# A polysketch attention and ELU kernel: one transpose placed five steps earlier, one outer product with a factor in PSUM, two of GpSimd's four sums in one operation

## The chip, the core and the metric

The kernel runs on one core of one Trainium2 chip. The metric is the time of one execution on the device in microseconds, taken as the median over runs. A core has these engines, each with its own instruction queue that is worked off in order: TensorE (PE in the profile, with its weight loads as PEld), VectorE (DVE), ScalarE (ACT), GpSimd (POOL), and SyncE (SP), which here only issues DMAs. They are tied together by semaphores: an instruction waits until the results and the buffers that it needs are there.

## What is computed

The reference, cut to what matters:

```python
batch, n_heads, seq, head_dim, r = 4, 4, 1088, 32, 8
def phi(x):                                   # 64 features of each row
    a = einsum('rd,bhsd->bhsr', S1, x)
    b = einsum('rd,bhsd->bhsr', S2, x)
    return einsum('bhsi,bhsj->bhsij', a, b).reshape(..., 64)
q_p, k_p = phi(q), phi(k)
kv = einsum('bhsf,bhsd->bhfd', k_p, v);  z = sum(k_p, axis=2)
num = einsum('bhsf,bhfd->bhsd', q_p, kv)
x = num / (einsum('bhsf,bhf->bhs', q_p, z) + 1e-6)
x = x.transpose(0, 2, 1, 3).reshape(4352, 128)    # heads side by side
h = x @ w_in                                      # 128 -> 2048
g = where(h > 0, h, exp(min(h, 0)) - 1)
out = g @ w_out                                   # 2048 -> 128
```

q, k and v are float32 in memory, S1, S2 and the weights float64 (two 32-bit words each). The kernel turns those to float32 itself as it needs them.

## The kernel before

**Two halves that run interleaved.** The second half, the two matrix products with the ELU between them, is most of the work. Its tokens are cut into nine groups g of 512 (the last one of 256), its 2048 hidden columns into eight pairs cp of 2 x 128. A step is one pair (g, cp). The list `steps` (lines 951 to 953) gives the order, and the loop at lines 1047 to 1087 works it off with the number n. The first half, the attention, supplies the input `xg` of each group just in time: its pieces hang on chosen steps.

**One step n** does, in the order of the instructions: `mm1` of (g, cp), two tiles `h` of 128 x 512 in PSUM; the extras given with `at(n, ...)`; `elu` of the first tile (on ScalarE `e` = relu(-h), then exp(-e), lines 808 and 810; on VectorE `gg` = max(e - 1, h), line 816); GpSimd's sums for it (`sums7`, c = 0); the extras given with `mid`; `elu` of the second tile; its sums (`sums7`, c = 1); the extras given with `late`; and last the second product of step n-2, `mm2`, `mm2_blocks` or `mm2_seven`. So a tile `gg` and its sums are used two steps after they are made. In steps where a group ends, that product comes ahead of the second `elu`.

**The seven products.** From group 2 on, and for two pairs of group 1, the second product is done with seven block products in place of eight (`mm2_seven`, line 723). It needs sums of the quarters of `gg`: with b11 and b12 the two halves of the first tile, b21 and b22 those of the second, GpSimd makes t0 = b12 - b11, t2 = b22 - b12, t1 = t2 + b11 and t3 = b21 - t1, each of 128 x 256 elements, in the tile `tt`. `SS` holds the matching sums of weights, made once by `weights7`. Most steps use the order t0, t2, t1, t3; the first and the last pair of a group use t1 first.

**The queries of a group** take this way, spread over steps: `transp` (line 279) transposes a batch's queries on VectorE from `hd_q` to `qT`; `queries(g5, g1, n)` (line 655) is one block of small matmuls on TensorE, the last product `q5` of group g5 and the first, `q1`, of group g1, into the two `h` tiles that the next step's `mm1` would use and two tiles `qps`; `q1_out` (line 541) brings q1's result to `abw` on VectorE; `q2_den` (line 555) makes the denominator and `an`, the first factor of the features divided by it, in four VectorE operations (`pw`, `den` twice, `an`; lines 560 to 570); `q2_half` (line 620) makes the outer product `qp` of `an` and the second factor; `q4` (line 628) transposes it to `qpT`, which `q5` uses. `q2_a` (line 614), where it is called, has ScalarE copy `an` into a PSUM tile `qa` first, and `q2_half` then reads its factor from there. In the kernel before this is so for groups 4 and 6; groups 2, 3 and 8 read `an` from SBUF. Group 2 and 3 belong to batch 1, groups 4 and 5 to batch 2.

**The keys of a batch** take a similar way: `transp` into `kT`, `KF_late` (matmuls into two `kfps` tiles), `KF_late_out` (two VectorE transposes to `abk`, line 369), the outer product `kp` in two halves (`KO_a`, `KO_b`), `KA` (matmuls into `kv`), and then `sums_out`, `turn` and `turned`, which end with `wz` on VectorE (line 453) and two small sums on GpSimd.

**PSUM slots.** `h` tiles rotate over four slots; `kfps`, `kv`, `ka`, `qa` and `qps` rotate over two slots named `aux`. A matmul that writes a rotated slot waits until the last reader of the slot's former tile is through. `queries` in step 22, for one, takes the slots of step 21's `h` and of `KF_late(3)`'s `kfps`.

Around the changed places the list of extras reads:

```python
late(n_f, KF_late_out, b)          # n_f = 6, 16, 21 for b = 1, 2, 3
at(21, transp, qT, "q", 2, 0, NT)
...
for n, g, nx in ((13, None, 2), (15, 2, 3), (22, 3, 4), (30, 4, 6), (46, 6, 8), (62, 8, None)):
    at(n, queries, g, nx, n + 1)
...
late(19, q2_den, 3)
late(19, q2_half, 3, 0)
late(20, q4, 3)
```

Of the kernel before, what the change touches and what calls it, by code (L numbers as in the profile page):

```python
# [15 lines left out]
MUL, ADD, SUB, MAX = ALU.mult, ALU.add, ALU.subtract, ALU.max  # L16
# [6 lines left out]
def _ap(ap: bass.AP, free):  # L23
    return dataclasses.replace(ap, ap=[list(ap.ap[0])] + [list(x) for x in free])
# [3 lines left out]
def kernel(  # L28
# [21 lines left out]
    nc = tc.nc  # L50
    B, H, S, D = q.shape
    R = S1.shape[0]
    P = 128
# [4 lines left out]
    NT = S // 64  # L58
# [14 lines left out]
    qT = [const.tile([FD, NT, 64], F32, name=f"qT{b}") for b in range(2)] * 2  # L73
# [593 lines left out]
    hs, es, gs, ops = {}, {}, {}, {}  # L667
# [19 lines left out]
    def quarter(g, cp, c, y):  # L687
        return gs[g, cp][:, c].rearrange("p (u x s) -> p u x s", u=2, x=2)[:, :, y, :]

    def sums7(g, cp, c):  # L690
        if c == 0:
            ts[g, cp] = work.tile([P, 4, 2, P], F32, name="tt", tag="raw", bufs=5)
        t = ts[g, cp]
        b11, b12 = (quarter(g, cp, 0, y) for y in range(2))
        if c == 0:
            nc.gpsimd.tensor_tensor(t[:, 0], b12, b11, op=SUB)  # L696
            return
        b21, b22 = (quarter(g, cp, 1, y) for y in range(2))
        nc.gpsimd.tensor_tensor(t[:, 2], b22, b12, op=SUB)  # L699
        nc.gpsimd.tensor_tensor(t[:, 1], t[:, 2], b11, op=ADD)  # L700
        nc.gpsimd.tensor_tensor(t[:, 3], b21, t[:, 1], op=SUB)  # L701

# [255 lines left out]
    def at(n, f, *a):  # L958
        extra.setdefault(n, []).append((f, *a))

    def mid(n, f, *a):
        extra.setdefault((n, 0), []).append((f, *a))

    def late(n, f, *a):
        extra.setdefault((n, 1), []).append((f, *a))
# [40 lines left out]
        at(n_z, turn, b)  # L1006
        at(n_z, turned, b)
    late(10, transp, qT, "q", 1, 0, NT)
    at(21, transp, qT, "q", 2, 0, NT)
    late(24, transp, qT, "q", 3, 0, NT)  # L1010

    for n, g, nx in ((13, None, 2), (15, 2, 3), (22, 3, 4), (30, 4, 6), (46, 6, 8), (62, 8, None)):
# [8 lines left out]
    late(13, q2_half, 2, 0)  # L1021
    mid(14, q4, 2)
    late(19, q2_den, 3)
    late(19, q2_half, 3, 0)
    late(20, q4, 3)
    late(22, q2_den, 4)
# [20 lines left out]
    for n in range(2, N):  # L1047
        g, cp = steps[n]
# [6 lines left out]
        if seven(g, cp):  # L1055
            sums7(g, cp, 0)
# [15 lines left out]
        if seven(g, cp):  # L1072
            sums7(g, cp, 1)
# [4 lines left out]
        g, cp = before  # L1078
# [10 lines left out]
    g = NQ - 2  # L1089
# [53 lines left out]
```

## Time and profile before

| | us |
|---|---|
| median of three runs | 264.04 |
| lowest, highest | 263.98, 265.52 |
| the profiled execution, its own time | 264.85 |
| its span, first to last instruction | 262.9 |
| TensorE busy | 257.1 |
| VectorE busy | 188.2 |
| ScalarE busy | 182.9 |
| GpSimd busy | 169.2 |
| GpSimd's four sums, 50 of each (lines 696, 699, 700, 701) | 36.7, 36.8, 36.6, 38.0 |

The granted clock of TensorE was 0.998 of full speed over the span. In the profile, step 15's `mm1` starts at 69.22 us, step 16's at 74.22, step 17's at 78.24, step 18's at 81.49, step 19's at 84.73, step 20's at 89.14, step 21's at 92.45, step 22's at 96.52 and step 23's at 102.48.

How to read the lines that follow. In a timeline a line gives start and length in us, engine, source line, operation, the tile written and the tiles read, shapes, how many instructions of the kind stand together, and in square brackets how long the engine stood idle before it and what ended that. VectorE's instructions overlap a little at their ends, so start to start is the better measure of a sequence. In a table of groups the last columns are busy time in us, mean length of one in ns, and idle time before them. The profile puts an idle time down to the instruction that released last by its records.

### The profile page before, as it was taken

The numbers are of one execution on the slowest core, as the hardware profiler recorded it, in microseconds if no ns is written. First come the engines' busy times: TensorE is split into PE (matmuls) and PEld (weight loads), VectorE is DVE, ScalarE is ACT, GpSimd is POOL, SyncE is SP. The second block draws the span as 40 slices with busy tenths as digits, with TensorE's granted clock in tenths as the row PEclk, the third lists the DMA queues.
The fourth block names the chain that finished last, engine by engine and source line by source line (L and its number), as shares of the span: only waits on it lengthen the run. The fifth ranks groups of instructions, "written<-read, shape, count | busy, mean of one in ns | idle before, by whom it ended". The sixth has DMA issues, their size and how long they took to land.

```text
span 262.9 us, 9941 instructions
## 1 busy us (share of the span) xinstructions
PE 257.1 (98%) x4219; PEld 159.2 (61%) x4219; DVE 188.2 (72%) x355; ACT 182.9 (70%) x356; POOL 169.2 (64%) x253
## 2 busy tenths in 40 slices
PE   8899999999999999999999999999999999999994
PEld 6652333354346746667666666665666666667994
DVE  5899999997969997996477676644456445673651
ACT  2469878677567655784687777776777777777793
POOL 4420008205387996798868799898689888997300
PEclk9999999999999999999999999999999999999999
DMA  5998079012011210001100200011001100110021
GB/s 171 326 353 220 7 235 268 7 36 78 12 24 26 33 38 3 5 15 26 35 0 4 30 13 2 0 29 15 5 0 17 27 4 0 24 21 2 0 32 33
DMA packets 28507, 14.30 MB, mean 54 GB/s; under 512 B 21392, under 2 KB 26640, under 8 KB 28464
## 3 DMA queue, kind: packets, MB, share of 16 engines
q1 hardware_dynamic: 28032, 13.32, 20.6%
q8 instruction: 33, 0.54, 0.9%
q10 hardware_dynamic: 368, 0.30, 0.3%
q14 instruction: 10, 0.08, 0.1%
q0 software_dynamic: 64, 0.07, 0.1%
HBM read 11.31 MB, written 2.36 MB: 52 GB/s over the span
## 4 chain that ended last, share of the span: by engine, by line
PE 94%; DMA 2%; DVE 1%; ACT 0%; issue 0%; ACTq 0%; DVEq 0%
PE h L256 45%; PE pb L737 17%; PE pa L737 13%; PE o L256 5%; PE pb L713 4%; PE ol L256 3%; DMA hd_k<-in_k_dram 2%; PE h L642 1%; PE kv L427 1%; PE qps L642 1%; PE kfps L359 1%; PE h L536 1%; PE qtp L595 1%; DVE qp L583 0%; PE xps L602 0%; PE abp L340 0%
## 5 line engine op out<-in xcount | busy, mean ns | idle before, releaser
L256 PE MATMUL h<-xg,W 128*32 128x512 f32 (+3 forms) x904 | 130.9, 540 | 0.4 <-ACT xg L608 0.4
L816 DVE SCALAR_TENSOR_TENSOR gg<-e,h 128x512 f32<-128x512 f32 x128 | 85.5, 682 | 52.6 <-ACT e L810 51.3
L808 ACT ACTIVATE e<-h 128x512 f32<-128x512 f32 x128 | 75.5, 590 | 47.0 <-PE h L256 46.0
L810 ACT ACTIVATE e<-e 128x512 f32<-128x512 f32 x128 | 80.9, 632 | 3.8
L256 PEld LDWEIGHTS h<-xg,W 128*32 128x32 f32 (+1 forms) x904 | 43.1, 122 | 43.2 <-issue 34.0
L699 POOL TENSOR_TENSOR tt<-gg 128x256 f32<-128x256 f32 x50 | 36.8, 737 | 16.3 <-DVE gg L816 16.1
L696 POOL TENSOR_TENSOR tt<-gg 128x256 f32<-128x256 f32 x50 | 36.7, 735 | 6.5 <-DVE gg L816 6.2
L701 POOL TENSOR_TENSOR tt<-gg,tt 128x256 f32<-128x256 f32 x50 | 38.0, 760 | 3.9
L700 POOL TENSOR_TENSOR tt<-tt,gg 128x256 f32<-128x256 f32 x50 | 36.6, 731 | 3.9
L737 PEld LDWEIGHTS pa<-gg,W 128*64 128x64 f32 (+1 forms) x496 | 23.9, 126 | 23.7 <-issue 23.0
L737 PE MATMUL pa<-gg,W 128*64 128x128 f32 (+1 forms) x496 | 30.7, 274 | 0.0
L737 PE MATMUL pb<-tt,SS 128*64 128x128 f32 (+1 forms) x480 | 29.6, 273 | 0.0
L737 PEld LDWEIGHTS pb<-tt,SS 128*64 128x64 f32 (+1 forms) x480 | 22.8, 126 | 0.0
L737 PE MATMUL pa<-tt,SS 128*32 128x128 f32 (+1 forms) x288 | 21.2, 273 | 0.0
L737 PE MATMUL pb<-tt,W 128*64 128x128 f32 (+1 forms) x256 | 20.2, 273 | 0.2 <-issue 0.2
L737 PE MATMUL pb<-gg,SS 128*64 128x128 f32 (+1 forms) x256 | 19.9, 273 | 0.0
L134 POOL TENSOR_TENSOR raw<-raw,tiny 128x512 f32<-128x512 f32 x1 | 1.0, 1042 | 24.7 <-DVE raw L129 24.7
L256 PE MATMUL o<-gg,W 128*32 128x512 f32 x128 | 15.3, 595 | 0.0
L737 PEld LDWEIGHTS pa<-tt,SS 128*32 128x32 f32 (+1 forms) x288 | 13.7, 124 | 0.0
L737 PEld LDWEIGHTS pb<-tt,W 128*64 128x64 f32 (+1 forms) x256 | 12.8, 125 | 0.5 <-issue 0.5
L737 PEld LDWEIGHTS pb<-gg,SS 128*64 128x64 f32 (+1 forms) x256 | 12.8, 125 | 0.0
L713 PE MATMUL pb<-gg,W 128*32 128x256 f32 x192 | 11.6, 380 | 0.0
(154 smaller groups left out, 285.2 us busy)
## 6 DMA issues: line engine op xcount, KB each, us to landing
raw<-in_moe_w_in_dram SPq DMA_DIRECT2D x8, 256.0 KB, 6.3
raw<-in_moe_w_out_dram SPq DMA_DIRECT2D x8, 256.0 KB, 6.6
out_dram<-ob SPq DMA_DIRECT2D x112, 16.0 KB, 1.5
hd_k<-in_k_dram SPq DMA_DIRECT2D x3, 544.0 KB, 6.8
hd_q<-in_q_dram SPq DMA_DIRECT2D x3, 544.0 KB, 8.2
v<-in_v_dram SPq DMA_DIRECT2D x4, 288.0 KB, 7.0
v<-in_v_dram SPq DMA_DIRECT2D x4, 256.0 KB, 8.6
kvs<-kvd SPq DMA_DIRECT2D x13, 32.0 KB, 1.9
```

The costliest lines, as they stand in the source:

```text
L256: nc.tensor.matmul(dst[c:c + tile], lhs[:, c:c + tile], rhs, skip_group_check=True, tile_position=(0, c), **kw)
L359: nc.tensor.matmul(ps[g2][32 * c:32 * c + 32, :32 * KT], Sxp[r].rearrange("p x c r -> p (x c r)"), kT[b][r, u * KT:u * KT + KT, 32 * w:32 ...
L642: nc.tensor.matmul(ps[w][32 * r:32 * r + 32, :64 * n], kvs[b][rows, r, f, :], qpT[g, i][rows, o:o + 2 * n, f, :], start=(f == 0), stop=(f ...
L696: nc.gpsimd.tensor_tensor(t[:, 0], b12, b11, op=SUB)
L699: nc.gpsimd.tensor_tensor(t[:, 2], b22, b12, op=SUB)
L700: nc.gpsimd.tensor_tensor(t[:, 1], t[:, 2], b11, op=ADD)
L701: nc.gpsimd.tensor_tensor(t[:, 3], b21, t[:, 1], op=SUB)
L713: nc.tensor.matmul(acc[1][0][r:r + width[0], 256 * hi:256 * hi + 256], lhs[:, w:w + width[0]], gg[:, c, 256 * u:256 * u + 256], start=(cp ...
L737: nc.tensor.matmul(bank[r:r + width[0], P * col:P * col + P], lhs[:, w:w + width[0]], rhs[:, u], start=(first and i in ((0,) if g == 1 els ...
L808: nc.scalar.activation(e, hs[g, cp][c][:, :n], RELU, scale=-1.0)
L810: nc.scalar.activation(e, e, EXP, scale=-1.0)
L816: nc.vector.scalar_tensor_tensor(gs[g, cp][:, c, :n], es[g, cp][:, c, :n], -1.0, hs[g, cp][c][:, :n], op0=ADD, op1=MAX)
```

## The change

Three edits. In `sums7` GpSimd does nothing after a step's first tile any more; after the second, one operation makes t0 and t2 together (128 x 512 elements: it reads b12 and b22 as the one operand, b11 and b12 as the other, and writes the slots 0 and 2 of `tt`), and t1 and t3 follow as before. The transpose of batch 2's queries is placed in step 16 in place of step 21; there it stands after the output transpose `ob` of group 0 and ahead of the two `gg` of step 16 on VectorE. And `q2_a` is called for group 3 in step 19, between `q2_den` and `q2_half`: ScalarE gets one copy more, in its queue behind the copy of `zl` and ahead of step 20's `e`, and it takes one `aux` slot, between batch 2's `kv` and batch 3's `kfps`. The order of all other instructions stays on every engine.

```diff
@@ sums7
         if c == 0:
             ts[g, cp] = work.tile([P, 4, 2, P], F32, name="tt", tag="raw", bufs=5)
         t = ts[g, cp]
-        b11, b12 = (quarter(g, cp, 0, y) for y in range(2))
         if c == 0:
-            nc.gpsimd.tensor_tensor(t[:, 0], b12, b11, op=SUB)
             return
-        b21, b22 = (quarter(g, cp, 1, y) for y in range(2))
-        nc.gpsimd.tensor_tensor(t[:, 2], b22, b12, op=SUB)
+        b11, b21 = quarter(g, cp, 0, 0), quarter(g, cp, 1, 0)
+        us = [[2 * P, 2], [1, P]]
+        nc.gpsimd.tensor_tensor(_ap(t[:, 0], [[4 * P, 2], [P, 2], [1, P]]), _ap(gs[g, cp][:, 0, P:], [[4 * P, 2]] + us),
+                                _ap(gs[g, cp][:, 0], [[P, 2]] + us), op=SUB)
         nc.gpsimd.tensor_tensor(t[:, 1], t[:, 2], b11, op=ADD)
         nc.gpsimd.tensor_tensor(t[:, 3], b21, t[:, 1], op=SUB)
@@ the extras
-    at(21, transp, qT, "q", 2, 0, NT)
+    at(16, transp, qT, "q", 2, 0, NT)
...
     late(19, q2_den, 3)
+    late(19, q2_a, 3, 0)
     late(19, q2_half, 3, 0)
```

## The prediction

> **What bounds the kernel now.** I read the page's engine shares and its chain first, since they say whose delay counts.
>
> ```profile
> PE 257.1 (98%) x4219; PEld 159.2 (61%) x4219; DVE 188.2 (72%) x355; ACT 182.9 (70%) x356; POOL 169.2 (64%) x253
> ...
> PE 94%; DMA 2%; DVE 1%; ACT 0%; issue 0%; ACTq 0%; DVEq 0%
> ```
>
> TensorE (PE) is busy 98% of the span and is 94% of the chain. None of the three edits touches a matmul, so they can win only where TensorE waits, and lose only where they make it wait. So I walked along TensorE's timeline and noted the length of each block from its start to the next block's start. In steps 16 to 62 an `mm1` takes 1.72 us and a `mm2_seven` 1.53 us, again and again. The blocks of `queries` differ. In step 15 (q5 and q1 both 128 columns wide) it runs from 71.06 to 72.47, 1.41 us; in step 30 (both 256 wide) from 128.81 to 130.87, 2.06 us; in step 46 (256 and 64) from 182.94 to 184.67, 1.73 us. In step 22 (128 and 256) it runs from 98.35 to 100.93, 2.58 us. The 96 matmul records of a block cost 0.65 us for 128 more columns, so 0.22 us for 32 of them. Step 46 confirms it: 2.06 less 32 records of 192 fewer columns (0.33) is 1.73. Step 22 should therefore take 1.41 + 0.22 = 1.63 us, and **0.95 us of it is a wait**. TensorE's weight loads in time order say for what:
>
> ```profile
> 98.34 0.38 PEld L642 LDWEIGHTS h<-qpT,kvs 32*32 32x32 f32 x4 [0.84 <-DVE gg L816]
> 98.98 0.13 PEld L642 LDWEIGHTS qps<-qpT,kvs 32*32 32x32 f32 x2 [0.26 <-DVE abk L369]
> 99.35 0.10 PEld L642 LDWEIGHTS qps<-qpT,kvs 32*32 32x32 f32 x1 [0.23 <-DVE abk L369]
> ```
>
> The block writes four PSUM tiles. The two `qps` take the slots of step 21's `kfps`, and those are free when VectorE (DVE) has run the two L369 transposes. The last comes free at 99.29, so the fourth load starts at 99.35 in place of 98.34. Now VectorE's timeline, to see why it is late:
>
> ```profile
> 89.58 0.24 DVE L436 STREAM_TRANSPOSE kvt<-kv 128x64 f32<-128x64 f32 x1
> 89.73 0.82 DVE L560 TENSOR_TENSOR pw<-abw 128x128 f32<-128x128 f32 x1
> 90.58 0.30 DVE L567 TENSOR_REDUCE den<-pw 128x16 f32<-128x144 f32 x1
> 90.92 0.25 DVE L568 RECIPROCAL den<-den 128x16 f32<-128x16 f32 x1
> 91.21 0.78 DVE L570 TENSOR_TENSOR an<-abw,den 128x128 f32<-128x128 f32 x1
> 92.02 1.71 DVE L625 TENSOR_TENSOR qp<-an,abw 128x1024 f32<-128x1024 f32 x1
> 93.65 0.18 DVE L453 TENSOR_TENSOR wz<-kv,bmask 128x32 f32<-128x32 f32 x1
> 93.75 1.27 DVE L816 SCALAR_TENSOR_TENSOR gg<-e,h 128x512 f32<-128x512 f32 x2
> 94.94 1.23 DVE L632 STREAM_TRANSPOSE qpT<-qp 128x1024 f32<-128x1024 f32 x1
> 96.11 1.27 DVE L280 STREAM_TRANSPOSE qT<-hd_q 128x1088 f32<-128x1088 f32 x1
> 97.30 1.24 DVE L816 SCALAR_TENSOR_TENSOR gg<-e,h 128x512 f32<-128x512 f32 x2
> 98.47 0.82 DVE L369 STREAM_TRANSPOSE abk<-kfps 128x288 f32<-128x288 f32 x2
> ```
>
> VectorE has no idle time here, and the 1.27 us transpose of batch 2's queries stands right ahead of the two `gg` and the two `abk` that TensorE waits for.
>
> **Edit 1, the transpose moved from step 21 to step 16.** It issues no DMA, and its data (load issued at 35.4) have long landed. In step 21, 1.2 us of the chain goes (from 96.11 to 97.30, start to start). In step 16 it stands behind the `ob` transpose, ahead of these two:
>
> ```profile
> 76.62 0.69 DVE L816 SCALAR_TENSOR_TENSOR gg<-e,h 128x512 f32<-128x512 f32 x1 [0.81 <-ACT e L810]
> 77.77 0.69 DVE L816 SCALAR_TENSOR_TENSOR gg<-e,h 128x512 f32<-128x512 f32 x1 [0.46 <-ACT e L810]
> ```
>
> It starts near 75.75 and ends near 77.03; the first `gg` slips from 76.62 to about 77.0 and ends at 77.7, and the second starts at 77.77 as before, since its input comes then. So step 16 costs nothing: 0.81 + 0.46 = 1.27 us of idle time takes it. Were this cover gone, steps 16 and 17 would lose up to 1.27 us on VectorE, and the first to feel it would be `fin_seven_a` of group 1 at 81.82, which TensorE's step 18 follows at 83.20.
>
> **Edit 2, `q2_a` for group 3.** ScalarE (ACT) copies `an` to PSUM (0.26 us by the four L618 rows), and `qp` reads it there. The rows of the two forms:
>
> ```profile
> L625 DVE TENSOR_TENSOR qp<-qa,abw 128x1024 f32<-128x1024 f32 x4 | 4.8, 1199 | 0.0
> L625 DVE TENSOR_TENSOR qp<-an,abw 128x1024 f32<-128x1024 f32 x2 | 2.9, 1466 | 0.1
> ```
>
> The two rows behind 1466 are 1.23 and this one's 1.71, so it gains 0.51 us here; the hand-over (copy and two semaphores, about 0.35) takes most of it. From the end of `an` (91.99) to the end of `wz` (93.83) is 1.84 us now; after, 0.35 + 1.20 + 0.18 + small change = 1.8. VectorE gains nothing, but ScalarE gains a wait: behind the copy in its queue stands `e` of step 20, which started at 90.28 and must now wait for `an`. Four operations of step 20 (2.41 us) follow, then `gg`.
>
> **Edit 3, one GpSimd (POOL) operation for two.** 512 elements on GpSimd have these rows:
>
> ```profile
> L134 POOL TENSOR_TENSOR raw<-raw,tiny 128x512 f32<-128x512 f32 x1 | 1.0, 1042 | 24.7 <-DVE raw L129 24.7
> ...
> L135 POOL TENSOR_TENSOR W<-raw,W 128x512 f32<-128x512 f32 x1 | 1.3, 1307 | 0.1
> ```
>
> Bounds are 1.04 and 1.47 us (two times 0.735, nothing saved). I take 1.30: the rows of 192, 256 and 1024 elements (0.60, 0.74, 2.19) lie on a line that gives it. A step of sums falls from 3.02 to about 2.9 us, but it starts only after the second `gg`: the last sum is ready 2.9 us after it in place of 2.35. TensorE doesn't feel it while slack lasts. In the steady steps the last sum would still end over 2 us ahead of its matmul; the tightest places are step 25 (sum `t1` at about 110.4, its matmul at 111.13: 0.7 us) and the tail (245.5 against 246.07: 0.57 us). At 1.47 us both still hold. So it costs nothing there.
>
> It reaches edit 2, though. In the rows above `pw` took 0.82 (0.28 in step 13, at 66.17) and `an` 0.78 (0.29): each began just after a GpSimd sum and ended 0.15 us after that sum's end, 90.40 and 91.84. A joined sum of 1.3 us is a longer thing to run into. In the new order GpSimd's join of step 19 would start about 90.8, and `an` about 90.8 too. If `an` gets in first it ends at 91.1, else at 92.25.
>
> The Trainium skill, SBUF — State Buffer (on the shared pair of ports), says that a VectorE instruction with two SBUF inputs and a GpSimd one lock each other out, and that the one which starts first holds the ports for its whole length. That speaks against joining; by it alone `an` would lose the tie, and the gain would be the lower end of the sum below. The row of `pw` fits the waiting but shows VectorE getting in when the running sum ends, though GpSimd's next one was ready to start (90.36).
>
> **The sum.** `an` first (91.1): `e` of step 20 runs 91.4 to 93.8, `gg` ends at 94.6, `qpT` at 95.7, step 21's `gg` at 97.0 (its `e` comes then), `abk` at 97.7. That is before TensorE arrives at 98.34, and the whole 0.95 us is won. `an` second (92.25): `e` 92.5 to 94.95, `gg` 95.7, `qpT` 96.85, `gg` 98.05, `abk` 98.85; the fourth load starts at 98.9 in place of 99.35, 0.45 us won. Step 21's `kfps` need `wz`, at 94.1 against 94.32: no stall. Behind step 22 TensorE's timeline shows no other wait for an engine, so what is won stays won. I take the middle, 0.7 us. Against the profiled execution (264.85 us, a span of 262.9 and 1.95 around it) that gives 264.15; this execution lies 0.8 above the median, and the same 0.7 off the median of 264.04 is **263.3 us**.
>
> **Rivals.** (a) The wait is exchanged, not removed: ScalarE's late `e` holds step 21's `gg` and `abk` until about 99.3. For it: the new wait of 2.2 us at 90.28. Against: edit 1 takes 1.2 us from the same chain. About 264.0. (b) Slower: both `pw` and `an` run into long sums, in place of one. It decides once `an` ends after 92.5, for then `wz` passes 94.32 and step 21's `kfps` stall; with one more wait of 1.3 us (`an` at 93.7) `wz` ends at 95.4, a stall of 1.1, and `abk` slips to 100.4. Price 1.0: 265.0 us. Against: only one join falls into this window. (c) The joined sum is much slower than its bounds: at the 2.19 us of 1024 elements, `t1` would be late by 0.2 to 0.4 us at each group's end. Little speaks for it; within 1 us, under 265.0.
>
> **How the numbers follow.** Forecast (0.4 to 1.0 us won) 0.6, (a) 0.22, (b) 0.13, (c) 0.05. No case reaches 1%, 2.6 us, which is about what a measurement of this kernel tells from no change; I leave 0.01 for faster and 0.04 for slower. The forecast's own range is 263.1 to 263.6. Below, a gap of 0.4 us without a releaser in TensorE's step 27 (119.7 to 120.2) may not come back: 262.7. Above, I go through (a) and most of the way to (b): 264.8.
>
> **What would show it.** Right: a `queries` block of step 22 of 1.6 to 2.1 us; no idle time left before `gg` in step 16; an `an` followed by a 1.2 us `qp`; joined sums of 1.3 us with no matmul waiting for `tt`. Wrong: a `kfps` load of step 21 that waits for `wz`, an `mm1` or `mm2_seven` of step 17 to 25 longer than 1.72 or 1.53, or `e` of step 20 starting after 92.7.

## The result

The changed kernel takes 263.44 us (median of 13 runs, 263.14 to 263.98), the kernel before 264.06 (13 runs, 263.75 to 265.76). The ratio is 0.9966, with a 95% interval of 0.9951 to 0.9982: faster by 0.34%, 0.9 us by the ratio (0.5 to 1.3) and 0.62 us by the medians. 0.7 us and 263.3 were forecast. In the terms of the forecast's chances this is within 1%.

The profiled execution after took 263.98 us, with a span of 262.1. The page's lines that answer to those shown of before, and GpSimd's joined sum in the table of groups:

```profile
PE 256.1 (98%) x4219; PEld 158.6 (61%) x4219; DVE 188.4 (72%) x355; ACT 183.1 (70%) x357; POOL 161.2 (62%) x203
...
PE 91%; DVE 5%; DMA 2%; issue 1%; ACT 0%; ACTq 0%; DVEq 0%
...
L698 POOL TENSOR_TENSOR tt<-gg 128x512 f32<-128x512 f32 x50 | 64.3, 1285 | 30.2 <-DVE gg L816 23.7 <-PE h L256 6.1
```

TensorE is 1.0 us less busy with the same 4219 matmuls, which fits waits that the profile had booked as long matmuls. VectorE's share of the chain, 5% now and 1% before, says nothing of step 22: the chain goes over VectorE from 40.60 to 49.95 us, a stretch in which TensorE's blocks have the same lengths in both kernels, and in step 22 it stays on TensorE. The run of edit 1 alone, below, has the same 5% with no wait in step 22. GpSimd is 8.0 us less busy (169.2 to 161.2), and the time has not followed that.

Where the time went is seen in the blocks of TensorE's timeline, from start to start. Of all blocks from step 2 to the end, three differ between the kernels by more than 0.05 us: the `queries` block of step 22 took 2.58 us before and takes 1.91 now (98.17 to 100.08), the `mm2_seven` of step 27 is 0.07 shorter, and the closing stretch with the last output is 0.09 longer. The other 0.18 us by which TensorE is ahead at step 15 came in the first 12 us, while the first loads land, and no edit touches that. So blocks tell more here than spans: in eight profiles of this study (before, after and the first six experiments) step 6's `kfps` start between 36.69 and 37.23 us.

TensorE's weight loads at the head of that block, in time order:

```profile
98.17 0.11 PEld L642 LDWEIGHTS h<-qpT,kvs 32*32 32x32 f32 x2 [0.84 <-DVE abk L369]
98.18 0.10 PEld L642 LDWEIGHTS qps<-qpT,kvs 32*32 32x32 f32 x1
...
98.50 0.10 PEld L642 LDWEIGHTS qps<-qpT,kvs 32*32 32x32 f32 x1 [0.19 <-DVE abk L369]
```

Three of the four tiles are free when TensorE arrives (the 0.84 ahead of the first load is the rest of the `mm1` before it, and stands there in every run). The fourth comes at 98.50 in place of 98.21 or so: 0.28 us of the wait is left of 0.95. VectorE's timeline of the changed kernel, first step 16 and then steps 19 to 21:

```profile
75.56 1.28 DVE L280 STREAM_TRANSPOSE qT<-hd_q 128x1088 f32<-128x1088 f32 x1
76.76 0.65 DVE L816 SCALAR_TENSOR_TENSOR gg<-e,h 128x512 f32<-128x512 f32 x1
77.59 0.69 DVE L816 SCALAR_TENSOR_TENSOR gg<-e,h 128x512 f32<-128x512 f32 x1 [0.18 <-ACT e L810]
...
89.55 0.42 DVE L560 TENSOR_TENSOR pw<-abw 128x128 f32<-128x128 f32 x1
...
90.63 1.38 DVE L570 TENSOR_TENSOR an<-abw,den 128x128 f32<-128x128 f32 x1
92.34 1.22 DVE L625 TENSOR_TENSOR qp<-qa,abw 128x1024 f32<-128x1024 f32 x1 [0.34 <-ACT qa L618]
93.49 0.18 DVE L453 TENSOR_TENSOR wz<-kv,bmask 128x32 f32<-128x32 f32 x1
93.60 0.69 DVE L816 SCALAR_TENSOR_TENSOR gg<-e,h 128x512 f32<-128x512 f32 x1
94.68 0.69 DVE L816 SCALAR_TENSOR_TENSOR gg<-e,h 128x512 f32<-128x512 f32 x1 [0.40 <-ACT e L810]
95.29 1.24 DVE L632 STREAM_TRANSPOSE qpT<-qp 128x1024 f32<-128x1024 f32 x1
96.45 1.25 DVE L816 SCALAR_TENSOR_TENSOR gg<-e,h 128x512 f32<-128x512 f32 x2
97.62 0.83 DVE L369 STREAM_TRANSPOSE abk<-kfps 128x288 f32<-128x288 f32 x2
```

In step 16 the transpose lies in time that was idle: the second `gg` still waits 0.18 us for its `e`. In step 21 it is gone. In step 19 `pw` takes 0.42 us (0.82 before) and `an` 1.38 (0.78 before), and there are two new waits, of `qp` for the copy (0.34) and of step 20's second `gg` for its `e` (0.40). Who holds `an` and whom it holds is seen on the other two engines, GpSimd and ScalarE:

```profile
90.58 1.27 POOL L698 TENSOR_TENSOR tt<-gg 128x512 f32<-128x512 f32 x1
...
92.04 0.27 ACT L618 COPY qa<-an 128x128 f32<-128x128 f32 x1 [3.89 <-DVE an L570]
92.25 0.59 ACT L808 ACTIVATE e<-h 128x512 f32<-128x512 f32 x1
```

The joined sum began 0.05 us ahead of `an`, and `an` ended 0.16 us after it. Behind the copy stands step 20's `e`, which begins at 92.25; before it began at 90.28.

### The profile page after: what moved, and what is told of

The parts are those of the page before. It is cut to its first block, busy times and chain, and to the rows that moved or that the text cites. A ratio compares the mean times of both kernels' runs of the same rounds, so it can differ in the third digit from the quotient of the medians.

```text
span 262.1 us, 9898 instructions
## 1 busy us (share of the span) xinstructions
PE 256.1 (98%) x4219; PEld 158.6 (61%) x4219; DVE 188.4 (72%) x355; ACT 183.1 (70%) x357; POOL 161.2 (62%) x203
## 4 chain that ended last, share of the span: by engine, by line
PE 91%; DVE 5%; DMA 2%; issue 1%; ACT 0%; ACTq 0%; DVEq 0%
PE h L256 43%; PE pb L737 17%; PE pa L737 13%; PE o L256 5%; PE pb L713 3%; PE ol L256 3%; DMA hd_k<-in_k_dram 2%; PE kv L427 1%; PE h L642 1%; DVE gg L816 1%; PE qps L642 1%; DVE raw L121 1%; PE kfps L359 1%; PE h L536 1%; PE qtp L595 1%
## 5 line engine op out<-in xcount | busy, mean ns | idle before, releaser
L698 POOL TENSOR_TENSOR tt<-gg 128x512 f32<-128x512 f32 x50 | 64.3, 1285 | 30.2 <-DVE gg L816 23.7
L701 POOL TENSOR_TENSOR tt<-gg,tt 128x256 f32<-128x256 f32 x50 | 36.9, 738 | 3.9
L868 DVE SCALAR_TENSOR_TENSOR gg<-e,h 128x256 f32<-128x256 f32 x16 | 6.6, 418 | 6.4 <-PE h L256 3.2
```

What stands on the lines that cost most here:

```text
L698: nc.gpsimd.tensor_tensor(_ap(t[:, 0], [[4 * P, 2], [P, 2], [1, P]]), _ap(gs[g, cp][:, 0, P:], [[4 * P, 2]] + us), _ap(gs[g, cp][:, 0], [[ ...
L868: nc.vector.scalar_tensor_tensor(gs["last", k // 2][:, k % 2, :2 * P], es["last", k // 2][:, k % 2, :2 * P], -1.0, hs["last", k][:, :2 * P ...
```

## The experiments

The theory: the gain is the wait of step 22 and edit 1 made it; edit 2 costs some of it, and edit 3 some more through `an`. The rivals: the shorter `qp` made it (the port theory), or GpSimd's relief did. Four kernels have one edit or two of the three; then the pair that was left, a third place for the transpose, and a measure of GpSimd's room.

### Edit 1 alone

```diff
-    at(21, transp, qT, "q", 2, 0, NT)
+    at(16, transp, qT, "q", 2, 0, NT)
```

> Edit 1 alone (the transpose in step 16; an in SBUF, four sums of GpSimd). Chain theory: the gain of the changed kernel is the wait of TensorE in step 22, and the transpose alone made it. Without the copy of an, ScalarE's e of step 20 starts near 90.3 again, so the two L369 transposes end near 98.1, before TensorE arrives: the queries block of step 22 takes 1.63 us (2.58 before, 1.91 in the changed kernel), and the time is 0.95 us below before, 0.3 below the changed kernel: about 263.1. Port theory (the shorter qp made the gain): block about 2.5, time as before. GpSimd theory (fewer operations made it): time as before.

Measured: 263.4 us (before beside it 264.25), ratio 0.997 (0.9959 to 0.998), 0.8 us faster. The block of step 22 takes 1.63 us, from 97.98 to 99.61, with no wait at its head. VectorE's timeline of this kernel:

```profile
91.64 1.71 DVE L625 TENSOR_TENSOR qp<-an,abw 128x1024 f32<-128x1024 f32 x1
...
94.56 1.23 DVE L632 STREAM_TRANSPOSE qpT<-qp 128x1024 f32<-128x1024 f32 x1
95.72 1.24 DVE L816 SCALAR_TENSOR_TENSOR gg<-e,h 128x512 f32<-128x512 f32 x2
96.89 0.82 DVE L369 STREAM_TRANSPOSE abk<-kfps 128x288 f32<-128x288 f32 x2
```

And the head of the block on TensorE:

```profile
97.98 0.11 PEld L642 LDWEIGHTS h<-qpT,kvs 32*32 32x32 f32 x2 [0.84 <-DVE abk L369]
97.99 0.11 PEld L642 LDWEIGHTS qps<-qpT,kvs 32*32 32x32 f32 x2
98.00 0.11 PEld L642 LDWEIGHTS h<-qpT,kvs 32*32 32x32 f32 x4
```

`qp` is as long as before, 1.71 us, and the gain is there, in the block all of it. The 0.3 us below the changed kernel that was expected as well shows in the block (1.63 against 1.91) and not in the time (ratios 0.997 and 0.9966). The port theory and the GpSimd theory fall as causes of the gain; 1.63 is also what the unwaited block was worked out to be. The transposes end at 97.71, 0.27 us ahead of TensorE's first load.

### Edit 2 alone

```diff
     late(19, q2_den, 3)
+    late(19, q2_a, 3, 0)
     late(19, q2_half, 3, 0)
```

> Edit 2 alone (an copied to PSUM for group 3; transpose in step 21, four sums). Chain theory: e of step 20 waits for an (ends near 92.0) and starts near 92.4; step 20's gg end near 95.7, qpT 96.9, the transpose 98.1, step 21's gg 99.3, the L369 transposes 100.1; TensorE's fourth load near 100.2 in place of 99.35: the block of step 22 takes about 3.4 us and the kernel is 0.8 us slower than before, about 264.9. Port theory: qp 0.5 us shorter, so the block is about 2.1 and the kernel 0.5 faster.

Measured: 264.45 us, ratio 1.0009 (1.0 to 1.0018); the block takes 2.87 us, 0.29 more than before. The sign is the theory's, the size a third of the expected 0.8. VectorE:

```profile
92.01 1.22 DVE L625 TENSOR_TENSOR qp<-qa,abw 128x1024 f32<-128x1024 f32 x1 [0.34 <-ACT qa L618]
...
94.35 0.69 DVE L816 SCALAR_TENSOR_TENSOR gg<-e,h 128x512 f32<-128x512 f32 x1 [0.39 <-ACT e L810]
94.95 1.24 DVE L632 STREAM_TRANSPOSE qpT<-qp 128x1024 f32<-128x1024 f32 x1
96.11 1.27 DVE L280 STREAM_TRANSPOSE qT<-hd_q 128x1088 f32<-128x1088 f32 x1
97.31 1.25 DVE L816 SCALAR_TENSOR_TENSOR gg<-e,h 128x512 f32<-128x512 f32 x2
98.48 0.83 DVE L369 STREAM_TRANSPOSE abk<-kfps 128x288 f32<-128x288 f32 x2
```

`qp` is 0.49 us shorter, and the chain ends later all the same, as ScalarE's `e` waits for `an`. The 0.5 us that was expected too much is spread over the chain: TensorE's timeline is 0.29 ahead here at step 22, and with that put back, `e` starts at 92.21 (92.4 expected), `gg` ends at 95.33 (95.7), the fourth load starts at 99.65 (100.2). So 0.19 us lies in the start of `e`, 0.18 between it and the end of `gg`, and the rest behind, where links of 1.2, 1.2, 1.2 and 0.8 us were expected and took 1.15, 1.19, 1.18 and 0.75 from end to end.

### Edit 3 alone

```diff
-            nc.gpsimd.tensor_tensor(t[:, 0], b12, b11, op=SUB)
...
-        nc.gpsimd.tensor_tensor(t[:, 2], b22, b12, op=SUB)
+        nc.gpsimd.tensor_tensor(_ap(t[:, 0], [[4 * P, 2], [P, 2], [1, P]]), _ap(gs[g, cp][:, 0, P:], [[4 * P, 2]] + us),
+                                _ap(gs[g, cp][:, 0], [[P, 2]] + us), op=SUB)
```

> Edit 3 alone (one operation for two sums; transpose in step 21, an in SBUF). Chain theory: GpSimd is about 8 us less busy and nobody waits for it, so the block of step 22 stays at 2.4 to 2.8 us and the time within 0.3 us of before; an still ends near 92.0, now held by one long operation in place of two short waits. GpSimd theory: the gain of the changed kernel, 0.6 us, appears here.

Measured: 264.51 us, ratio 1.0004 (0.9995 to 1.0014): no difference. The block takes 2.79 us, 0.21 more than before. VectorE:

```profile
89.39 0.42 DVE L560 TENSOR_TENSOR pw<-abw 128x128 f32<-128x128 f32 x1
...
90.47 1.40 DVE L570 TENSOR_TENSOR an<-abw,den 128x128 f32<-128x128 f32 x1
```

`an` takes 0.62 us more than before, since it began 0.04 us after the start of a joined sum (90.43 to 91.71). `pw` takes 0.40 less, since it met a sum (88.93 to 89.66) near its end. The difference of the two is the price. So the join by itself wins nothing, and has a small price through `an` that the interval doesn't resolve.

### Edits 1 and 3

The two diffs above together; `an` stays in SBUF.

> Edits 1 and 3 without the copy of an. Chain theory: as with edit 1 alone, block of step 22 at 1.63 us, 0.95 us below before, about 263.1, thus 0.3 faster than the changed kernel. Port theory: without the factor in PSUM qp runs into GpSimd's longer operations and the time is no better than before.

Measured: 263.2 us, ratio 0.9959 (0.9947 to 0.9971); the block takes 1.63 us, though `an` takes 1.40 and `qp` 1.71 here:

```profile
90.25 1.40 DVE L570 TENSOR_TENSOR an<-abw,den 128x128 f32<-128x128 f32 x1
91.69 1.71 DVE L625 TENSOR_TENSOR qp<-an,abw 128x1024 f32<-128x1024 f32 x1
...
96.95 0.82 DVE L369 STREAM_TRANSPOSE abk<-kfps 128x288 f32<-128x288 f32 x2
```

This kernel's block is 0.28 us shorter than the changed kernel's. The two ratios overlap, so the times do not tell them apart; the block does.

### Edits 1 and 2

> Edits 1 and 2, GpSimd's four sums left apart. The changed kernel's an was held 1.38 us by one joined sum; with four sums it should end some 0.3 us earlier, as in the run of edit 2 alone. Theory: of the 0.28 us of step 22's wait that is left in the changed kernel, the longer GpSimd operation makes about 0.2 and the copy of an the rest: block of step 22 at 1.65 to 1.75 us (1.91 in the changed kernel, 1.63 without the copy), time 0.1 to 0.3 below the changed kernel. Rival: the copy alone makes the wait, and the block stays at 1.9.

Measured: 263.42 us, ratio 0.9972 (0.9961 to 0.9982); the block takes 1.71 us, `an` 0.77. The rival (1.9 from the copy alone) falls. The time was expected 0.1 to 0.3 us below the changed kernel; the ratios, 0.9972 and 0.9966, do not show that. All seven combinations that were run now stand by the length of step 22's block, in us:

| transpose in | neither | copy | join | both |
|---|---|---|---|---|
| step 21 | 2.58 | 2.87 | 2.79 | not run |
| step 16 | 1.63 | 1.71 | 1.63 | 1.91 |

The upper row gives the price of the copy as 0.29 and of the join as 0.21. In the lower row VectorE is ahead of TensorE, by some 0.2 us (0.27 from the transposes' end to the first load, less the hand-over), and only what passes that shows: 0.29 - 0.21 = 0.08 for the copy, nothing for the join, 0.29 + 0.21 - 0.22 = 0.28 for both. One slack of 0.21 to 0.22 us explains all three. The times resolve none of the differences within the lower row: the ratios to the kernel before are 0.997, 0.9972, 0.9959 and 0.9966, and their intervals overlap.

### The transpose in step 19

```diff
-    at(16, transp, qT, "q", 2, 0, NT)
...
+    late(19, transp, qT, "q", 2, 0, NT)
     late(19, q2_den, 3)
```

> The changed kernel with the transpose of batch 2's queries in step 19, ahead of pw, in place of step 16. Theory: what counts is that it stands where VectorE has idle time, not that it has left step 21. In step 19 VectorE has none: an ends near 92.9, wz near 94.6, so step 21's kfps load waits 0.3 to 0.6 us for it, and the L369 transposes end near 99.4: block of step 22 about 2.4 us; time 0.8 to 1.2 above the changed kernel, about 264.4. Rival (it only had to leave step 21, as the data of q1 come from there): as the changed kernel, 263.4.

Measured: 264.41 us, ratio 1.0007 (0.9997 to 1.0016), 1.0 above the changed kernel. VectorE and the two places at which TensorE waits, in this kernel's timeline:

```profile
89.15 1.31 DVE L280 STREAM_TRANSPOSE qT<-hd_q 128x1088 f32<-128x1088 f32 x1
90.35 1.25 DVE L560 TENSOR_TENSOR pw<-abw 128x128 f32<-128x128 f32 x1
...
94.16 0.28 PEld L359 LDWEIGHTS kfps<-kT,Sxp 64*32 64x32 f32 x16 [1.27 <-DVE qp L625]
...
99.04 0.10 PEld L642 LDWEIGHTS qps<-qpT,kvs 32*32 32x32 f32 x1 [0.23 <-DVE abk L369]
```

Here the prediction's slower rival is seen at work: step 21's `kfps` load waits 0.43 us longer than elsewhere (1.27 against 0.84) for `qp` and `wz`, and step 22's block still takes 2.33 us. The transpose has left step 21, and against the kernel before nothing is won: what counts is where it goes. (The changed kernel differs in the place alone. The kernel before lacks edits 2 and 3 as well, and the kernel with these two and the transpose in step 21 was not run, so what step 19 wins or costs against step 21 is not shown.) `pw` ran into the joined sum (90.18 to 91.45) and ended at 91.60.

### One sum more on GpSimd

```diff
         nc.gpsimd.tensor_tensor(t[:, 1], t[:, 2], b11, op=ADD)
+        nc.gpsimd.tensor_tensor(t[:, 1], t[:, 2], b11, op=ADD)
```

> The changed kernel with the sum t1 made twice in every step. It measures how far GpSimd is from being the bound: a step of sums takes about 2.9 us and 3.7 with one sum more, against 3.25 us of TensorE in the steady steps. Theory: some 34 steps each run 0.45 us over, less about 2 us of slack: 10 to 20 us slower, TensorE waiting for tt. Rival (the sums are hidden by two steps of lag whatever they take): no change.

Measured: 277.61 us in one run, 14 above the changed kernel. GpSimd is now half of the chain that the page follows back from the end:

```profile
POOL 50%; PE 37%; DVE 5%; issue 4%; ACT 2%; DVEq 0%; POOLq 0%
```

and TensorE's waits have two rows that no other kernel here has (us in total, how often, longest):

```profile
PE pa L738 <- POOL tt L701: 3.9, 11, 1.1
PE pb L738 <- POOL tt L702: 3.5, 15, 0.5
```

Its steps come 3.66 us apart (joined sums at 182.32, 185.98, 189.65), and so do TensorE's (3.24 before). The sums stay hidden only while those of a step take less time than TensorE's step: 2.90 us in the changed kernel (87.72 to 90.62, step 18's) are hidden, 3.66 are not. The rival, that the lag of two steps hides them whatever they take, falls.

## Why the prediction was right, and where it was off

**What bounds the kernel, and the wait of 0.95 us in step 22**: shown. The unwaited block was put at 1.63 us from three other blocks, and edit 1 alone runs it in 1.63.

**Edit 1**: shown, in size as well, and step 16 is free of cost; 0.18 us of its idle time is left, where the prediction expected none. Step 19 as a third place shows that the idle time in step 16 was needed.

**Edit 2**: the ledger was right in kind. `qp` took 1.22 us, `an` to `wz` 1.66 (1.84 before, 1.8 forecast), and the wait of step 20's `e` was there, from 90.1 to 92.25. Its price by itself is 0.29 us.

**Edit 3**: the joined sum takes 1.285 us (1.30 forecast), and no matmul waits for `tt`. The three rows from which 1.30 was read do not lie on one line: those of 192 and 256 elements lead to 1.30 at 512, those of 256 and 1024 to 1.22. That `an` would run into it was put as a tie with two outcomes; it came out as the second, `an` ending at 92.0 (92.25, or 92.07 in this execution's time, forecast). The rule of the Trainium skill, SBUF — State Buffer (SBUF: two separate sides, on the shared pair of ports), had said that the one which starts first holds it, and so it went: the sum began at 90.58 and `an` at 90.63. In the run with the transpose in step 19 `pw` began inside a joined sum and waited for its end in the same way.

**The sum**: the number came out for a reason that is in part luck. I took 0.7 as the middle of 0.45 (`an` second) and 0.95 (`an` first). `an` was second, and the block still won 0.67. The term that was mis-sized is the chain behind `an`: forecast in this execution's time, `gg` of step 20 ends at 95.5, `qpT` at 96.7, step 21's `gg` at 97.9, the transposes at 98.7 and the fourth load starts at 98.7; measured 95.4, 96.5, 97.7, 98.45 and 98.50. Most of the 0.22 us lies ahead of the end of `gg`: `an` ended 0.06 earlier than forecast, and from there to the end of `gg` it took 3.36 us in place of 3.45. The links behind, forecast at 1.15, 1.20 and 0.80 us, took 1.16, 1.17 and 0.75. The prediction also held about 1% to be what a measurement of this kernel tells from no change; these runs tell 0.34%, with an interval of 0.18 to 0.49%.

**"What is won stays won"**: shown. Behind step 22 every block but that `mm2_seven` of step 27 and the closing stretch has its old length within 0.05 us.

**The rivals**: (a), that ScalarE's late `e` takes back the gain, happened with 0.28 of 0.95 us, together with the join. (b) did not happen; the run with the transpose in step 19 shows its stall of step 21's `kfps` to be real, though there one operation ran into a long sum and not two. (c) did not: 1.285 us lies within the bounds. The low end of the range counted on a gap in step 27 that might not come back; it came back nearly whole. The `mm2_seven` of that step, 1.53 us elsewhere, takes 1.98 us before and 1.91 in this profile; in those of the first six experiments it takes 1.90, 1.75, 1.96, 1.63, 1.62 and 1.53, in the order above. It follows no edit, and its cause is open; it alone can move a profiled execution by 0.4 us, more than edit 2 or edit 3 costs.

## What to carry to other kernels

When one engine is busy nearly all the time, compare its blocks of one kind with each other: a block that is longer than its shape explains holds a wait that the busy share hides. Then follow the waited-for engine back to an operation that nobody needs yet, and put it where that engine has idle time, which must be looked for; the same move to a step without idle time, in a kernel with all three edits, won nothing against the kernel before. Edits that shorten an operation or relieve an engine off that chain can still cost, through what they put in front of others in a queue: two of the three edits here were worth nothing or less.

## What was not expected

How regularly VectorE and GpSimd hold each other; that `an` could be held as long as this had been forecast. `an` of 128 x 128 took 0.29 us free of GpSimd (step 13), 0.78 beside a sum of 256 elements, and 1.38 to 1.40 beside the joined one, ending 0.14 to 0.16 us after it each time. In the run with the transpose in step 19 it began at 92.26, 0.07 us ahead of a sum, and took 0.29. GpSimd is held in turn: the last sum of step 19 takes 1.59 to 1.60 us in the four kernels whose `qp` reads two tiles in SBUF (before, edit 1, edit 3, edits 1 and 3), and 0.73 to 0.81 where one factor is in PSUM (the changed kernel, edit 2, edits 1 and 2, the transpose in step 19). The longer operation saves GpSimd 0.16 us a step (8.0 us over 50) that nobody waits for, and in step 19 of the run with edit 3 alone it costs VectorE 0.2 us that TensorE waits for.
